# Chunked attention and a snake MLP in one kernel: the first batch's loads move to GpSimd, its units become even and odd blocks, its constants move to VectorE and ScalarE

## The chip, the cores and the metric

The kernel runs on one core of one Trainium2 chip. Its time is device microseconds of one execution; runs are summed up by their median. A profile is taken of one further execution: it shows five engines (TensorE as PE with its weight loads as PEld, VectorE as DVE, ScalarE as ACT, GpSimd as POOL, and SyncE as SP, which here only starts DMAs), 16 DMA engines that all queues share, and the clock that TensorE was granted. A "span" is the time from the first to the last instruction in the profile; the execution's own time is a little longer.

## The reference

Two parts, the second on the output of the first. Attention has batch 4, 8 heads, 768 rows and 64 columns a head; each chunk of 32 queries sees 16 rows to the left of its chunk, its own 32 and 8 to the right, and 8 memory rows of its batch:

```python
k_full = concatenate([mem_k, k[l_start:r_end]]); v_full = concatenate([mem_v, v[l_start:r_end]])
a = softmax(q_c @ k_full.T / sqrt(64))
out[c_start:c_end] = a @ v_full
```

The heads are laid side by side, which gives x of 3072 x 512. The MLP is

```python
h = x @ w_in                     # 512 -> 2048
s = sin(alpha * h)
g = h + s * s / (alpha + 1e-9)
y = g @ w_out                    # 2048 -> 512, float32, 3072 x 512
```

All inputs and the output are float32; the kernel computes the matmuls in bfloat16.

## The kernel before, in words

Everything is staged by batch. While the MLP of batch i runs on TensorE, the attention of batch i + 1 is worked in between. A first stage, number -1, has only the attention of batch 0 and the constants. What every engine does, and in which order, is written out by hand: `WORDS` holds one string for each stage, and each word calls one method of `Stage` (`do_` and the word's first letter). Every engine works through its own instructions in that order, so a wait of one instruction holds all behind it on its engine. There is no planner.

Words of the first stage that matter here, with what they issue:

- `k0` to `k3`, `l0` to `l3`: TensorE transposes a pair of heads of K or Q (`turn`, 12 matmuls each). `K1V`, `L0A`: the pair is copied from PSUM to its place by VectorE (V) or ScalarE (A).
- `s10`: scores of one unit (`u_scores`): head pair 1, half 0. A unit is two heads by four blocks of 96 queries. Two matmuls write the mask as a product of `mrow` and `mind`, eight add the scores, and ScalarE takes the exponential into a `pt` tile.
- `v10`: values of that unit (`u_values`, 8 matmuls), then `normed` on VectorE: a reciprocal of the sums and a product.
- `t10`, `T10`: four transposes and one copy of the result into xT, by VectorE or ScalarE.
- `V024`: V rows of heads 2 and 3 of batch 0 (`load_v`), two GpSimd DMAs that cast to bfloat16. V is kept in windows of 128 rows for each of 8 blocks: 64 rows, 8 memory rows, 56 rows.
- `dq068`: a pair of Q by GpSimd with a cast (`load_one`). `I02`, `I27`, `U69`: pieces of w_in and w_out, also by GpSimd.
- `a4A`: a cast of a float32 pair (`kq_f`) to bfloat16, by ScalarE.
- `C` and a letter: a group of constants (`const_b` and so on).
- `y1`, `z1`: fillers, TensorE matmuls on zeros (four of 128 columns, one of 512).

In the MLP's stages `b3` and `h3` are the two halves of the first layer's tile 3 (4 matmuls of 384 columns each, L457) with the sine on ScalarE after the second, `q3A` is the square, `g3` joins them on VectorE (L484), and `f6` takes six matmuls of the second layer (L495) from a queue.

The loads of batch 0 go two ways. Three of four pairs of K and of Q come as float32 on the queues of SP (K) and ScalarE (Q) into `kq_f`, and are cast by ScalarE or VectorE (`do_a`, L686). The fourth pairs and all of V come through GpSimd, which casts on the way. GpSimd, before its first load, writes the identity, zero rows of V's windows and `mind`. The first unit of a head pair takes blocks 0 to 3 and the second blocks 4 to 7, so V is needed whole by pairs. The program lets eight DMAs of GpSimd be in flight: each issue waits for the one eight before it.

The output of a batch is written by `close` in `second`: one DMA on SP for every 128 rows (L505).

Of the kernel before, what the change touches and what calls it, by code (L numbers as in the profile page):

```python
# [9 lines left out]
P = 128  # L10
QW = 96
# [15 lines left out]
    ),  # L27
    (
# [93 lines left out]
def kernel(  # L122
# [49 lines left out]
    pts = [consts.tile([P, H * QW + 32], BF, name=f"pt{i}") for i in range(NPT)]  # L172
# [6 lines left out]
    memk_bf = memv_st[0:NK, 0]  # L179
    memk_st = memv_st[96:104].rearrange("n b h d -> n b (h d)")  # L180
    memkT = consts.tile([P, HP, NK], BF, name="memkT")
# [36 lines left out]

    def win(vflat, row, n, height):
        a = vflat[row:row + 1, :]  # L220
        return bass.AP(tensor=a.tensor, offset=a.offset, ap=[[D, height], [QW * D, n], [1, D]])
# [20 lines left out]
    def put_memk(b):  # L242
        nc.vector.tensor_copy(
            kTs[b % 2][:, :, 24:856].rearrange("p g (j c) -> p g j c", c=104)[:, :, :, 40:40 + NM],
            memkT[:, :, NM * b:NM * b + NM].unsqueeze(2).to_broadcast([P, HP, NJ, NM]),
        )
# [100 lines left out]
    def u_scores(b, hp, half):  # L347
        t, bs = banks.pair()
        for e in range(2):
            nc.tensor.matmul(  # L350
                t[:, e, 0:HALF], mrow[64 * e:64 * e + 64, :],
                mind[64 * e:64 * e + 64, 4 * half:4 * half + 4].rearrange("p j m c -> p (j m c)"),
                start=True, stop=False,
            )
        for i in range(4):
            j = 4 * half + i
            for e in range(2):
                nc.tensor.matmul(
                    t[:, e, QW * i:QW * i + QW],
                    kTs[b % 2][64 * e:64 * e + 64, hp, 104 * j:104 * j + P],  # L360
                    qTs[b % 2][64 * e:64 * e + 64, hp, QW * j:QW * j + QW],
                    start=False, stop=(i == 3),
                )
        pt = next_pt()
        nc.scalar.activation(  # L365
            pt[:, 0:H * QW].rearrange("p (e c) -> p e c", e=2), t[:, :, 0:HALF],
            ACTF.Exp, scale=0.125,
        )
        banks.give(bs)
        return pt  # L370

    def u_values(b, hp, half, pt):
        ot, bs = banks.pair()
        otv = ot[:, :, 0:4 * (D + 1)].rearrange("p e (g c) -> p e g c", c=D + 1)
        for e in range(2):
            for i in range(4):
                nc.tensor.matmul(
                    otv[:, e, i, :], pt[:, HALF * e + QW * i:HALF * e + QW * i + P],
                    vws[b % 2][:, 2 * hp + e, 4 * half + i, 0:D + 1],
                )  # L380
        return normed(otv, bs)
# [109 lines left out]
    def second(i, gT, group=0):  # L491
# [8 lines left out]
        def close(o, bs, s, c0=0, c1=d_model):  # L500
# [4 lines left out]
            nc.sync.dma_start(out[S * i + P * s:S * i + P * s + P, c0:c1], o_sb[:, c0:c1])  # L505
# [30 lines left out]
    class Stage:  # L536
# [139 lines left out]

        def do_H(self, a):
            put_memv_heads(int(a))
# [3 lines left out]

        def do_a(self, a):
            hp = int(a[0]) % HP
            dst = kq[int(a[0]) // HP]
            copier(a[1])(  # L686
                dst[:, 2 * hp:2 * hp + 2].rearrange("p h r d -> p h (r d)"), kq_f[int(a[0])][:]
            )
# [53 lines left out]
    kq_f = [mlp.tile([P, 2, 6 * D], F32, name="kq_f", tag=t) for t in ("u", "s2") * 4]  # L742
# [3 lines left out]

    def load_f(ring, src, hp, t):
        ring.dma_start(
            t[:], src[0, 2 * hp:2 * hp + 2].rearrange("h (p r) d -> p h (r d)", p=P)
        )  # L750
# [5 lines left out]
    for hp in range(HP - 1):  # L756
        load_f(nc.sync, k, hp, kq_f[hp])
        load_f(nc.scalar, q, hp, kq_f[4 + hp])
        if hp == 0:
            nc.sync.dma_start(memv_f[64:72], mem_v[0].rearrange("h n d -> n h d"))  # L760
    nc.vector.memset(zeros[:], 0.0)
    nc.vector.memset(tiny[:], 0.0)
    nc.vector.memset(mcol[:], 0.0)
    masks.make_identity(nc, ident[:])
    for vw in vws:
        nc.gpsimd.memset(vw[0:32, 0, 0, 0:D], 0.0)
        nc.gpsimd.memset(vw[96:128, H - 1, NJ - 1, 0:D], 0.0)
# [29 lines left out]
    def const_i():  # L797
        nc.gpsimd.tensor_tensor(out=asum[:, 0:5], in0=ident[:, 0:5], in1=ident[:, 64:69], op=ALU.add)
        nc.gpsimd.tensor_tensor(out=asum[:, 5:7], in0=asum[:, 0:3:2], in1=asum[:, 3:5], op=ALU.add)
        nc.gpsimd.tensor_copy(  # L800
            mind[:], asum[:, 0:3].unsqueeze(1).unsqueeze(3).to_broadcast([P, NJ, 3, 32])
        )
        nc.gpsimd.tensor_copy(mind[:, 0, 0, :], asum[:, 5:6].to_broadcast([P, 32]))
        nc.gpsimd.tensor_copy(mind[:, NJ - 1, 2, :], asum[:, 6:7].to_broadcast([P, 32]))

    def const_k():
        nc.vector.tensor_copy(memk_bf, memk_f[0:NK])
        bank, bs = banks.single()
        mt = bank[:, 0:2 * NK].bitcast(BF).rearrange("p (g c) -> p g c", g=HP)
        for g in range(HP):  # L810
            nc.tensor.transpose(
                mt[:, g, :], memk_bf[:, 2 * g:2 * g + 2, :].rearrange("p e d -> p (e d)"),
                ident[0:NK, 0:NK]
            )
        nc.vector.tensor_copy(memkT[:], mt)
        put_memk(0)
        if not CROSSED[1][0]:
            put_memk(1)
        banks.give(bs)

    def const_f():
        nc.vector.tensor_copy(memv_st[64:72, 0], memv_f[64:72])

    def const_l():
        nc.vector.tensor_copy(ident_f[:], ident[0:FT, 0:FT])
# [7 lines left out]
    def const_z():  # L833
        for kT in kTs:
            nc.gpsimd.memset(kT[:, :, 0:16], 0.0)
            nc.gpsimd.memset(kT[:, :, 848:856], 0.0)

    def const_p():
        for pt in pts:
            nc.gpsimd.memset(pt[:, H * QW:H * QW + 32], 0.0)  # L840

    def const_v():
        for vw in vws:
            nc.gpsimd.memset(vw[:, :, :, D:D + 1], 1.0)

    def const_s():
# [3 lines left out]
    consts_of = dict(b=const_b, f=const_f, m=const_m, i=const_i, k=const_k, l=const_l, p=const_p, v=const_v,  # L850
                     s=const_s, z=const_z)
# [37 lines left out]
```

## Time and profile before

| | us |
|---|---|
| median of 3 runs | 214.56 |
| lowest and highest | 214.24, 215.09 |
| the profiled execution's own time | 214.68 |
| its span | 212.8 |

| engine | busy us | share of the span |
|---|---|---|
| PE | 204.9 | 96% |
| ACT | 143.7 | 68% |
| DVE | 139.9 | 66% |
| POOL | 100.9 | 47% |

In a row of a timeline come the start in us from the span's start, the length in us, the engine (a small q behind it is its sequencer, which starts DMAs), the line of the code, the operation with out<-in, shape and count, and in brackets how long the engine stood idle before and what ended that. In a row of the waits come who waited, for whom, and the total in us, the times and the longest. In a group's row come busy time in us and the mean of one in ns, and after the second bar idle time before them. In a row of DMA issues come the queue, the count, the size of each at its destination, and the us from issue to landing. In a row of a DMA queue come packets, MB written, and the time of its packets as a share of 16 engines.

### The profile page before, as it was taken

The page shows a single profiled execution, that of the slowest core. Times are in us where ns is not written, and L with a number is a line of the kernel's source. Part 1 is how long each engine was busy: PE and PEld are TensorE (multiplying, and loading weights), DVE is VectorE, ACT ScalarE, POOL GpSimd, SP SyncE. Part 2 cuts the span into 40 slices and gives each one's busy share as a digit, 9 for nine tenths or more (in the row PEclk, how much of TensorE's full clock was granted, in tenths as well). Part 3 has the DMA queues.
Part 4 walks back from the last instruction along what each step waited for, and adds up shares of the span by engine and source line. Part 5 has one row for each costly group of instructions (what it writes and reads, how often), then busy time and mean ns, then how long its engine had stood idle before and what let it go on. Part 6 is the DMA issues. An engine that isn't in the chain of part 4 may idle for free.

```text
span 212.8 us, 4568 instructions
## 1 busy us (share of the span) xinstructions
PE 204.9 (96%) x1772; PEld 118.1 (55%) x1772; DVE 139.9 (66%) x210; ACT 143.7 (68%) x229; POOL 100.9 (47%) x142
## 2 busy tenths in 40 slices
PE   7879999999999999999999999999999999999994
PEld 7456665565455556555455555554555555554453
DVE  4788788999452749976766649897247187865010
ACT  2579898978848469968837199887856189891110
POOL 8998605589697297109795048664000022200000
PEclk9999999999999999999999999999999999999999
DMA  5999999999999999999999259999944400000312
GB/s 156 332 158 139 212 207 204 205 139 183 131 160 155 176 114 129 121 144 146 146 152 183 74 125 125 137 157 133 134 104 107 137 0 0 3 2 0 148 52 99
DMA packets 95853, 27.82 MB, mean 131 GB/s; under 512 B 84808, under 2 KB 92376, under 8 KB 95832
## 3 DMA queue, kind: packets, MB, share of 16 engines
q0 software_dynamic: 69152, 13.64, 89.3%
q1 hardware_dynamic: 25720, 12.68, 29.6%
q10 hardware_dynamic: 960, 1.21, 1.7%
q8 instruction: 14, 0.23, 0.6%
q14 instruction: 7, 0.06, 0.1%
HBM read 29.66 MB, written 6.29 MB: 169 GB/s over the span
## 4 chain that ended last, share of the span: by engine, by line
PE 78%; DVE 8%; ACT 5%; DMA 4%; issue 3%; SPq 1%; DVEq 0%; ACTq 0%
PE ps L495 39%; PE ps L457 30%; DMA kq_f<-in_k_dram 4%; PE ps L447 3%; DVE gT L484 2%; PE ps L418 2%; DVE x_blk L387 2%; DVE s L480 2%; ACT s L477 2%; PE ps L399 1%; ACT pt L365 1%; PE ps L312 1%; ACT u L472 1%; DVE q_bf L686 1%; DVE rinv L386 0%
## 5 line engine op out<-in xcount | busy, mean ns | idle before, releaser
L495 PE MATMUL ps<-w_out_sb,gT 128*128 128x512 bf16 (+1 forms) x400 | 89.1, 371 | 0.0
L457 PE MATMUL ps<-xT,w_in_sb 128*128 128x384 bf16 x512 | 85.9, 326 | 0.6 <-DVE gT L484 0.4
L484 DVE SCALAR_TENSOR_TENSOR gT<-s,inv_alpha,ps 128x768 bf16<-128x768 f32 x64 | 63.1, 1012 | 12.3 <-ACT s L477 5.2
L457 PEld LDWEIGHTS <-w_in_sb 128*128 128x128 bf16 x512 | 49.7, 98 | 35.2 <-issue 2.0
L472 ACT ACTIVATE u<-ps,alpha_sb 128x768 f32<-128x768 f32 x64 | 56.6, 894 | 16.9 <-PE ps L457 14.4
L495 PEld LDWEIGHTS <-gT 128*128 128x128 bf16 x400 | 37.1, 98 | 37.1 <-DVE gT L484 0.2
L480 POOL TENSOR_TENSOR s<-u 128x768 f32<-128x768 f32 x11 | 17.2, 1568 | 67.2 <-ACT u L472 56.4
L432 ACT ACTIVATE pt<-ps,biasm 128x256 bf16<-128x256 f32 x72 | 27.1, 488 | 10.5 <-PE ps L418 10.5
L502 DVE COPY o_sb<-ps 128x512 f32<-128x512 f32 (+1 forms) x15 | 10.0, 669 | 27.6 <-PE ps L495 25.7
L480 DVE TENSOR_TENSOR s<-u 128x768 f32<-128x768 f32 x23 | 21.9, 953 | 7.6 <-ACT u L472 7.5
L477 ACT ACTIVATE s<-u 128x768 f32<-128x768 f32 x30 | 25.0, 841 | 0.5
L387 DVE TENSOR_TENSOR x_blk<-ps,rinv 96x512 bf16<-96x512 f32 x32 | 22.0, 687 | 1.1
L502 ACT COPY o_sb<-ps 128x512 f32<-128x512 f32 (+1 forms) x10 | 5.7, 572 | 22.0 <-PE ps L495 22.0
L208 POOL DMA_DIRECT2D vw<-in_v_dram x13 | 12.0, 926 | 6.3 <-PE ps L399 5.4
L386 DVE RECIPROCAL rinv<-ps 96x8 f32<-96x8 f32 x32 | 6.4, 199 | 13.1 <-PE ps L447 12.7
L215 POOL DMA_DIRECT2D vw<-in_v_dram x13 | 13.3, 1024 | 1.6 <-DMA vw<-in_v_dram 1.6
L274 POOL DMA_DIRECT2D kst<-in_k_dram x16 | 13.0, 815 | 1.8 <-DMA vw<-in_v_dram 1.2
L268 POOL DMA_DIRECT2D kst<-in_k_dram x16 | 11.1, 691 | 2.1 <-DMA kst<-in_k_dram 1.0
L281 POOL DMA_DIRECT2D q_bf<-in_q_dram x12 | 10.7, 911 | 0.0
L402 ACT COPY xT<-ps 128x384 bf16<-128x384 bf16 x10 | 5.0, 496 | 8.2 <-PE ps L399 8.2
L447 PEld LDWEIGHTS <-pt 128*128 128x128 bf16 x192 | 8.2, 97 | 4.2 <-ACT pt L432 0.3
L447 PE MATMUL ps<-vw,pt 128*128 128x65 bf16 x192 | 8.9, 193 | 0.0
(83 smaller groups left out, 140.7 us busy)
## 6 DMA issues: line engine op xcount, KB each, us to landing
out_dram<-o_sb SPq DMA_DIRECT2D x23, 256.0 KB, 2.2
q_bf<-in_q_dram POOLq DMA_DIRECT2D x12, 128.0 KB, 7.7
kq_f<-in_k_dram SPq DMA_DIRECT2D x3, 384.0 KB, 6.2
kq_f<-in_q_dram ACTq DMA_DIRECT2D x3, 384.0 KB, 7.9
w_in_sb<-in_moe_w_in_dram POOLq DMA_DIRECT2D x1, 1152.0 KB, 12.9
vw<-in_v_dram POOLq DMA_DIRECT2D x7, 128.0 KB, 7.7
vw<-in_v_dram POOLq DMA_DIRECT2D x8, 112.0 KB, 8.1
kst<-in_k_dram POOLq DMA_DIRECT2D x14, 64.0 KB, 5.5
```

What stands on the lines that cost most here:

```text
L215: nc.gpsimd.dma_start(vw[72:128, c0:hi, 0:D], win(vflat, base + QW * c0 + 48, hi - c0, 56))
L274: nc.gpsimd.dma_start(kst[72:72 + n, j, :].rearrange("p (h d) -> p h d", d=D), k[b, :, QW * j + 48:QW * j + 48 + n, :].rearrange("h p d -> ...
L387: nc.vector.tensor_tensor(out=x_blk[:].rearrange("p g e d -> p e g d"), in0=otv[0:QW, :, :, 0:D], in1=rinv[:].unsqueeze(3).to_broadcast([Q ...
L432: nc.scalar.activation(pt[:, 0:H * QW].rearrange("p (g e c) -> p g e c", g=2, e=4)[:, :, :, 32 * m:32 * m + 32], sc[:, :, 0:4 * QW].rearra ...
L447: nc.tensor.matmul(otv[:, e, hp, :], pt[:, QW * i:QW * i + P], vws[b % 2][:, 2 * hp + e, j, 0:D + 1],)
L457: nc.tensor.matmul(t["hT"][:, hf, 0:HALF], w_in_sb[:, kt, P * t["ft"]:P * t["ft"] + P], t["xT"][:, kt, HALF * hf:HALF * hf + HALF], start= ...
L472: nc.scalar.activation(t["u"][:], t["hT"][:, :, 0:HALF], ACTF.Sin, scale=alpha_sb[:, ft:ft + 1])
L477: nc.scalar.activation(s2[:], u[:], ACTF.Square)
L480: e.tensor_tensor(out=s2[:], in0=u[:], in1=u[:], op=ALU.mult)
L484: nc.vector.scalar_tensor_tensor(out=gT[:, ft, :].rearrange("p (e c) -> p e c", e=2), in0=t["s2"][:], scalar=inv_alpha[:, ft:ft + 1], in1= ...
L495: nc.tensor.matmul(o[:, c0:c1], gT[:, ft, P * s:P * s + P], w_out_sb[:, ft, c0:c1], start=(ft == 0), stop=(ft == FT - 1),)
L502: copier(state["engines"][state["o"] % len(state["engines"])])(o_sb[:, c0:c1], o[:, c0:c1])
```

## The change

It touches stage -1, the words of stage 0, and the output's row order of batch 0.

- All pairs of K and Q of batch 0 are loaded by GpSimd with the cast, in the order pair by pair with V; the first load is POOL's first instruction. The float32 tiles, the loads on SP and ScalarE, and the casts go.
- The two units of a head pair are the even and the odd blocks. The last pair's V is loaded in such halves (`load_v_half`, words `G030` and `G031`). xT of batch 0 holds the even blocks first, and `close` puts the rows back in order with two DMAs for each 128 rows.
- `asum`, the identity's memset, and the zeros and ones that batch 0 needs are made by VectorE, `mind` by ScalarE; those of batch 1 stay on GpSimd and come later (`Cw`, `Cy`). The eight `pt` tiles become one, so that one memset serves them.
- Memory keys are transposed as float32 and go from PSUM straight to kT; memory values go from float32 to V's windows by pairs (`put_memv_first`, words `n0A` and so on) instead of a cast and one broadcast copy.
- The words of stages -1 and 0 are ordered anew, with fewer fillers: 44 of 128 columns and one of 512 in place of 48 and 14.

```diff
-        'y1 y1 y1 Ci y1 a4A We y1 Cb a1A y1 y2 y1 y1 dq068 Cl y1 Cm y1 Cf z1 z1 eVA z1 eVA a0A Ck m0 Cz z1 '
-        'dk068 Cp V024 z1 z1 V002 z1 a2V V068 z1 z1 Cv l0 z1 a5V z1 L0A k1 k0 z1 k2 l1 K1A V046 K0A a6V L1A '
-        's00 s10 s11 K2V l2 k3 L2V K3A s01 v11 dm l3 L3A v10 s20 v01 s30 v00 s31 v30 s21 v31 z1 T01 v20 T30 '
-        'I02 Cs T00 v21 t10 T20 t31 z1 t11 I27 t21 Ws '
+        'Cv Cp Cb dk002 dq024 y1 y1 Ci We y1 dk024 y1 y1 y1 n0A y1 k0 K0A V002 Cz y1 Cd y1 n1V dq046 dk046 Ck '
+        'Cm l0 L0A k1 s00 l1 V024 s01 K1V L1V v00 y1 n3A s10 v01 l2 k2 n2A T01 s11 K2V dq068 dk068 z1 V046 '
+        'L2V G030 T00 v10 y1 v11 s20 l3 s21 k3 L3V K3V Cw T10 v20 s30 G031 v21 Cy I02 s31 v30 T11 v31 t20 T21 '
+        'I27 Cs Ws t30 Cl dm t31 '
...
-        'o8 b0 h0 I7g q0V U69 U12 b1 h1 dq108 q1A b4 h4 b3 g0 h3 b6 g1 dk108 q4V g4 q3A b2 h2 h6 b5 h5 Ufg g3 '
-        'b7 q2V U01 U56 q6P h7 g2 q5A b10 U24 q7P g6 h10 b9 q10A g5 h9 U45 b8 h8 g7 g10 q8A q9V V158 b11 h11 '
+        'o8 b0 h0 I7g q0V U69 U12 Ws b1 h1 dq108 q1A b3 b4 g0 h4 h3 b6 g1 q4V g4 q3A dk108 b2 h2 h6 b5 h5 Ufg '
+        'g3 b7 q2V U56 q6P h7 g2 q5A b10 U24 q7P g6 U01 h10 b9 q10A g5 h9 U45 b8 h8 g7 g10 q8A q9V V158 b11 '
...
+    def load_v_half(b, hp, half):
...
+        c0 = 2 * hp * NJ + half
...
+        c1 = (2 * hp + 2) * NJ
+        for c, r0, r1 in ((lo, 0, 64), (c0, 72, 128)):
+            row = b * H * S + QW * c - 16 + (r0 if r0 == 0 else 64)
+            a = vflat[row:row + 1, :]
+            nc.gpsimd.dma_start(
+                vw[r0:r1, c:c1:2, 0:D],
+                bass.AP(tensor=a.tensor, offset=a.offset,
+                        ap=[[D, r1 - r0], [2 * QW * D, (c1 - c + 1) // 2], [1, D]]))
...
-                mind[64 * e:64 * e + 64, 4 * half:4 * half + 4].rearrange("p j m c -> p (j m c)"),
+                mind[64 * e:64 * e + 64, half:NJ:2].rearrange("p j m c -> p j (m c)"),
...
-            j = 4 * half + i
+            j = 2 * i + half
...
+            if i:
+                nc.sync.dma_start(out[S * i + P * s:S * i + P * s + P, c0:c1], o_sb[:, c0:c1])
+                return
+            r = 0
+            while r < P:
+                at = P * s + r
+                n = min(P - r, QW - at % QW)
+                g = at // QW
+                row = QW * (2 * (g % 4) + g // 4) + at % QW
+                nc.sync.dma_start(out[row:row + n, c0:c1], o_sb[r:r + n, c0:c1])
+                r += n
...
-    for hp in range(HP - 1):
-        load_f(nc.sync, k, hp, kq_f[hp])
-        load_f(nc.scalar, q, hp, kq_f[4 + hp])
...
+    nc.vector.memset(ident[:], 0.0)
+    load_one(q, q_bf, 0, 0, 2)
+    masks.make_identity(nc, ident[:], nomemset=True)
...
+        nc.scalar.copy(mind[:], asum[:, 0:3].unsqueeze(1).unsqueeze(3).to_broadcast([P, NJ, 3, 32]))
...
-        nc.vector.tensor_copy(memkT[:], mt)
-        put_memk(0)
...
+        for b in range(B):
+            if not CROSSED[b][0]:
+                put_memk(b, mt, "V")
```

More of the change, by code (lines that the diff above doesn't have):

```diff
@@ L171 @@
     NPT = 8
-    pts = [consts.tile([P, H * QW + 32], BF, name=f"pt{i}") for i in range(NPT)]
+    pt_all = consts.tile([P, NPT, H * QW + 32], BF, name="pt")
+    pts = [pt_all[:, i] for i in range(NPT)]
     memv_st = consts.tile([P, B, H, D], BF, name="memv_st")
@@ L675, in do_m, with do_n, do_G @@
             put_memv(int(a))
+        def do_n(self, a):
+            put_memv_first(int(a[0]), a[1])
+        def do_G(self, a):
+            load_v_half(*(int(c) for c in a))
         def do_H(self, a):
@@ L797, in const_i, with const_d @@
     def const_i():
[L798 to L804, printed above, removed]
+        nc.vector.tensor_tensor(out=asum[:, 0:5], in0=ident[:, 0:5], in1=ident[:, 64:69], op=ALU.add)
+        nc.vector.tensor_tensor(out=asum[:, 5:7], in0=asum[:, 0:3:2], in1=asum[:, 3:5], op=ALU.add)
+        nc.scalar.copy(mind[:], asum[:, 0:3].unsqueeze(1).unsqueeze(3).to_broadcast([P, NJ, 3, 32]))
+        nc.scalar.copy(mind[:, 0, 0, :], asum[:, 5:6].to_broadcast([P, 32]))
+        nc.scalar.copy(mind[:, NJ - 1, 2, :], asum[:, 6:7].to_broadcast([P, 32]))
+    def const_d():
+        nc.vector.tensor_copy(ident_f[:], ident[0:FT, 0:FT])
     def const_k():
[L807 removed]
         bank, bs = banks.single()
[L809 removed]
+        mt = bank[:, 0:HP * NK].rearrange("p (g c) -> p g c", g=HP)
         for g in range(HP):
             nc.tensor.transpose(
[L812 to L818 removed]
+                mt[:, g, :], memk_f[0:NK, 2 * g:2 * g + 2, :].rearrange("p e d -> p (e d)"),
+                ident_f[0:NK, 0:NK]
+            )
+        for b in range(B):
+            if not CROSSED[b][0]:
+                put_memk(b, mt, "V")
         banks.give(bs)
[L821 to L822 removed]
     def const_l():
[L825 removed]
         bank, bs = banks.single()
```

65 lines of the change are left out of this document (31 added, 34 removed), and 6 rows, old and new, of the table WORDS.

## The prediction

> **What bounds the kernel now.** I read the page first, then the waits of TensorE over the whole run, the chain in order of time, and the timelines of the first 45 us.
>
> ```profile
> span 212.8 us, 4568 instructions
> ...
> PE   7879999999999999999999999999999999999994
> ```
> ```profile
> PE ps L725 <- DVE tiny L762: 1.2, 1, 1.2
> PE ps L312 <- DVE q_bf L686: 1.0, 1, 1.0
> PE ps L811 <- DVE memv_st L807: 0.9, 1, 0.9
> ```
> ```profile
> 2.57 8.45 DMA kq_f<-in_k_dram
> ...
> 14.60 2.22 ACT pt L365 x3
> ...
> 24.95 2.62 PE ps L457 x16
> ```
> ```profile
> 1.20 4.45 PE L725 MATMUL ps<-zeros 128*128 128x128 bf16 x40 [1.20 <-DVE tiny L762]
> ...
> 8.29 1.47 PE L719 MATMUL ps<-zeros 128*128 128x512 bf16 x6
> ...
> 10.69 0.86 PE L312 MATMUL ps<-ident,k_bf 128*64 128x128 bf16 x24
> ...
> 19.08 0.34 PE L350 MATMUL ps<-mind,mrow 64*128 64x384 bf16 x2
> 19.25 0.33 PE L358 MATMUL ps<-qT,kT 64*128 64x96 bf16 x8
> 19.52 0.43 PE L377 MATMUL ps<-vw,pt 128*128 128x65 bf16 x8
> ...
> 24.78 17.40 PE L457 MATMUL ps<-xT,w_in_sb 128*128 128x384 bf16 x104
> ```
> ```profile
> 26.28 0.90 ACT L472 ACTIVATE u<-ps,alpha_sb 128x768 f32<-128x768 f32 x1
> ```
>
> The three largest waits of TensorE come to 3.1 us of a 212.8 us span, and all three lie in the first batch's preparation. The chain starts with 8.45 us of waiting for K's float32 loads, passes to the exponentials at 14.60, and reaches the first layer (L457) at 24.95; the timeline has that layer from 24.78 with 104 matmuls in 17.40, 167 ns each, without a gap. Behind it the slices stand at 9 to the end. So some 188 us are a queue of matmuls that no other engine holds up, and the time is the moment at which the first layer starts plus those 188. The change keeps the matmuls of the three later batches and all MLP matmuls. What it is worth is how far the first layer moves. Its first tile has 8 matmuls (24.78 + 8 x 0.167 = 26.1), and the first sine follows at 26.28; that is the mark I work out.
>
> **The loads.** Four groups of rows, POOL's timeline and the DMA view of single issues:
>
> ```profile
> 1.03 0.29 POOL masks.py:199 TENSOR_SCALAR_AFFINE_SELECT ident<-ident 128x128 bf16<-128x128 bf16 x1
> ...
> 3.66 0.94 POOL L191 DMA_DIRECT2D q_bf<-in_q_dram  x1
> ...
> 6.91 0.89 POOL L215 DMA_DIRECT2D vw<-in_v_dram  x1
> 7.78 0.56 POOL L204 DMA_DIRECT2D vw<-in_v_dram  x1
> ...
> 15.78 0.81 POOL L249 DMA_DIRECT2D w_in_sb<-in_moe_w_in_dram  x1
> ```
> ```profile
> q_bf<-in_q_dram POOLq DMA_DIRECT2D x1, 192.0 KB, 7.8
> ```
> ```profile
> w_in_sb<-in_moe_w_in_dram POOLq DMA_DIRECT2D x1, 256.0 KB, 6.9
> ```
> ```profile
> w_in_sb<-in_moe_w_in_dram POOLq DMA_DIRECT2D x1, 640.0 KB, 8.1
> ```
> ```profile
> vw<-in_v_dram POOLq DMA_DIRECT2D x1, 64.0 KB, 2.6
> ```
> ```profile
> q0 software_dynamic: 543, 0.41, 131.5%
> ```
> ```profile
> q0 software_dynamic: 2514, 0.30, 241.6%
> ```
>
> The last two are GpSimd's queue in two stretches of 2 us: rows of Q at 35 to 37 (0.41 MB, 205 KB a us) and rows of V at 12 to 14 (0.30 MB, 150 KB a us). A pair of heads of K or Q (192 KB) thus takes 0.95 us of DMA, all eight 7.6. V (64 blocks of 120 rows of 128 B, 0.98 MB) takes 6.6; I take 7.9, since it slowed in the stretch after. Together 15.5 us.
>
> POOL's program now opens with the first load of Q at 0.75, where it had its identity. Issues cost 0.94 at most, 0.85 on average; the identity slips in between (0.29). Ahead of the last V half stand 4 x 0.85 + 0.29, the 48-row V load 0.56, then two K/Q pairs of 1.7, six V issues of 0.88, four half-block issues that have no row and lie between 0.56 and 0.89 (I take 0.7), and two memsets (0.65): it is issued by 17. DMA work starts about 2.0 (below) and needs 15.5, so POOL and the DMA engines end together: last K/Q pair landed by 14, the last V by 18.6, w_in's first part (issued about 17.3) by 20.1, against 15.78 + 6.9 = 22.7 before. The in-flight limit on this queue (each issue waits for the one eight earlier) finds landings one to five us old.
>
> How long the first issue waits for its first packet has no clean row. The 64 KB V load at 73.3, into a quiet queue, landed after 2.6; the first Q load of before, behind six float32 loads on the other queues, after 7.8. I take the near end, since those six are gone: Q's first pair lands at 3.4, K's at 4.5. The far end is a rival.
>
> **The compute of the first batch.** Durations by form, 0 to 26 us:
>
> ```profile
> L365 ACT ACTIVATE pt<-ps 128x768 bf16<-128x768 f32 x8 | 6.3, 822 | 0.2 <-PE ps L358 0.2
> L387 DVE TENSOR_TENSOR x_blk<-ps,rinv 96x512 bf16<-96x512 f32 x8 | 5.5, 687 | 0.3
> ...
> L332 ACT COPY qT<-ps 128x768 bf16<-128x768 bf16 x3 | 2.5, 819 | 1.4 <-PE ps L312 1.4
> ...
> L386 DVE RECIPROCAL rinv<-ps 96x8 f32<-96x8 f32 x8 | 1.6, 198 | 0.4 <-PE ps L377 0.4
> ...
> L402 DVE COPY xT<-ps 128x384 bf16<-128x384 bf16 x4 | 1.1, 344 | 0.0
> ...
> L332 DVE COPY qT<-ps 128x768 bf16<-128x768 bf16 x1 | 1.0, 958 | 0.6 <-PE ps L312 0.6
> L323 DVE COPY kT<-ps 128x768 bf16<-128x768 bf16 x1 | 0.9, 939 | 0.0
> ...
> L800 POOL COPY mind<-asum 128x768 bf16<-128x768 bf16 x1 | 0.8, 818 | 0.0
> ...
> L822 DVE CAST memv_st<-memv_f 8x512 bf16<-8x512 f32 x1 | 0.6, 584 | 0.0
> ```
> ```profile
> 3.33 0.24 POOL L803 COPY mind<-asum 128x32 bf16<-128x32 bf16 x1
> ```
> ```profile
> 7.14 0.20 ACT L738 ACTIVATE tiny<-zeros 1x1 f32<-1x1 bf16 x1
> ```
> ```profile
> 1.35 0.75 DVE L773 TENSOR_REDUCE biasm<-ident 128x1 f32<-128x56 bf16 x6
> ...
> 3.35 0.15 DVE L786 TENSOR_TENSOR mcol<-biasm 128x2 bf16<-128x2 f32 x1
> ```
>
> *Constants.* The identity is ready at 0.75 + 0.94 + 0.29, about 2.05, where it was 1.35. VectorE's mask constants (1.35 to 3.5, 2.15 us) end at 4.2, two additions for asum (as L786, 0.15 each) at 4.5. Then ScalarE writes mind: 0.82 on POOL, taken the same, plus two small copies of 0.24 and the exponential's warm-up of 0.2: 6.05. Its first memory-value copy (8 partitions x 1024, float32) has no row; twice L822 gives 1.17, a 128x768 ScalarE copy scaled by size 1.1; below it cannot be free, so 0.5 to 1.2, and I take 1.1: 7.15. K's first pair goes out at 7.15 to 7.9, Q's to 8.7. The data has been there since 4.5 and the transposes (24 in 0.86) since 7, so late loads have 1.2 us of slack. The GpSimd constants taken away (mind, 8 pt memsets, vw, kT) cost POOL nothing now; their replacements on VectorE before 2.05 hide behind the wait for the identity. The casts (L686) go; nothing takes their place but these two copies.
>
> *First unit.* Its scores take 0.34 (L350 and L358, each 0.17 from start to start) and end at 9.1, its exponential 0.8 (9.9). The transposes of Q's second pair stand behind these scores in TensorE's order, so VectorE copies it from 9.55 to 10.5.
>
> *VectorE from 10.5 on* has its work queued without a gap that I can find: eight units of 0.69 + 0.20 + 0.03 (0.92, 7.4 us) and four copies of K and Q pairs (0.95, 3.8 us): 21.7. Then three copies to xT (0.36 with issue) and alpha's copy and reciprocal (0.42): 23.2. ScalarE beside it has from 9.1 eight exponentials (6.4), two memory copies (2.2) and three xT copies (1.5) ahead of the last unit's values: 20.0 with its waits, 0.4 ahead of VectorE's need. The last V half (18.6) is 1.5 ahead of its use, w_in's first part (20.1) 2 ahead. So VectorE, not the loads, ends the stage. TensorE's first tile ends at 23.4 against 26.1: **2.7 us earlier.**
>
> *Later.* w_in's next part, issued behind it, lands about 23.3 (before 17.64 + 8.1 = 25.7); it is wanted at 22.1 + 16 x 0.167 = 24.8. The loads behind it move with it by some 2.5. Batch 0's output takes twelve issues on SP instead of six; they stand ahead of the DMA transposes of batch 1 in SP's order, but each waits for a copy that TensorE's 16 matmuls release, so SP has time between them: nothing. If that cover is gone, the transposes of c6, c4 and c2 are what comes late. The even/odd order in matmul operands is a stride on 96-column runs: nothing.
>
> Sum: the profiled execution took 214.68, 1.9 over its span and 0.12 over the median of the runs shown (214.56); 214.68 - 2.7 = 212.0, which I give also against the median.
>
> **The rivals.**
>
> *Late first packet.* If GpSimd's first load needs the far end's wait, everything that arrives moves by 3.2; 1.2 is slack, 2.0 is paid: gain 0.7, 214.0. For it: the 7.8. Against it: six loads on other queues stood before that one.
>
> *The weights do not move.* If w_in's second part still lands at 25.7, TensorE waits 0.9 to 1.1 at its third tile: gain 1.6, 213.1. Against it: the same bytes, begun earlier.
>
> *TensorE stays slow: slower than before.* The first 40 fillers took 111 ns per 128 columns, the later ones 245 per 512, 61 per 128: at the start TensorE runs at about half pace. After the change 28 fillers end at about 4.3, and then TensorE waits for K's first pair; if it stays at half pace until 12, the eight blocks of work there on which VectorE waits (five transposes of 0.45, three scores of 0.34, two values of 0.4 (L377), 4.1 us) double: about +4.0, less the 2.7 gained: 216.0. It decides from 2.7 us of such loss on. For it: twelve 512-column fillers are gone. Against it: K lands at 4.5, and from there to 7 TensorE has work.
> The Trainium skill, "TensorE: Matmul & The Clock Gate", Part 1, says that the clock is halved by default, comes up after a busy window of about 3.4 us and falls back after an idle one. The 111 and 61 ns agree with its two states; by that rule a gap shorter than the window would cost nothing, and with late loads the gap would be as long as the window.
>
> *It does nothing.* If VectorE's work runs a quarter longer, because in the new order it reads PSUM beside ScalarE and TensorE all the time, its 11.2 us become 14.0 and the gain is gone: 214.8. In the rows above its eight units ran beside ScalarE's exponentials already, at 0.69.
>
> **How the numbers follow.** 0.5% is 1.07 us, about what a measurement of this kernel tells from no change. My forecast (gain 1.8 to 3.8, 210.9 to 212.8) has 0.52; weights not moving 0.12; late packet or nothing gained 0.19; slow TensorE 0.17. So faster 0.64, same 0.19, slower 0.17. The unknown copies (0.5 to 1.2, three of them, two off the path) and half-block issues set the low end: 210.8. The high end, 215.8, reaches into the slow case.
>
> **What would show it.** Right: first K transposes by 5.5, first exponential about 9, VectorE without gaps from 10.5 to 23, first-layer matmuls from about 22 without a gap, a load of w_in landed by 20.5, granted clock 1.0 throughout. Wrong: Q's first packet after 5 us; granted clock 0.5 after 6 us; TensorE waiting for DMA in the first layer; GpSimd issues above 1 us.

## The result and the profile after

| | before | after |
|---|---|---|
| median, us (same chip) | 214.82 | 217.12 |
| lowest and highest | 214.24, 215.33 | 216.69, 217.39 |
| ratio to before, with its 95% interval | | 1.0106 [1.0071, 1.0140] |
| the profiled execution, and its span | 214.68, 212.8 | 216.69, 214.9 |

The change makes the kernel about 1% slower, where 2.7 us less was forecast. Measured again beside other kernels it took 216.24, ratio 1.0075 [1.0042, 1.0109]. A ratio is to the kernel before on the same chip, with its 95% interval, and leaves out executions more than 1.5% above their kernel's fastest, so it can differ a little from that of two medians.

The line of the clock from the profile's page, and the first 16 us of TensorE's timeline:

```profile
PEclk9669999999999999999999999999999999999999
```
```profile
1.21 2.99 PE L758 MATMUL ps<-zeros 128*128 128x128 bf16 x28 [1.21 <-DVE zeros L784]
6.79 0.53 PE L336 MATMUL ps<-ident,k_bf 128*64 128x128 bf16 x12 [2.60 <-DMA k_bf<-in_k_dram]
7.25 1.03 PE L758 MATMUL ps<-zeros 128*128 128x128 bf16 x8
8.22 0.60 PE L834 MATMUL ps<-ident_f,memk_f 16*128 16x16 f32 x4
8.75 0.29 PE L816 MATMUL ps<-ident,mcol 128*128 128x128 bf16 x1
8.97 0.85 PE L336 MATMUL ps<-ident,q_bf 128*64 128x128 bf16 x12
...
15.01 0.50 PE L336 MATMUL ps<-ident,k_bf 128*64 128x128 bf16 x12
```

TensorE stands idle for 2.60 us until K's first pair lands. Twelve transposes take 0.53 us at 6.79, 0.85 at 8.97 and 0.50 again at 15: between 7.3 and 14.1 it runs at half pace, the two sixes in the clock's line. Q's first transposes come 2.2 us behind K's, since eight fillers, the memory keys and a constant stand between them in TensorE's order.

GpSimd's timeline and the DMA view of its first two loads and of w_in's first part:

```profile
1.27 0.93 POOL L190 DMA_DIRECT2D q_bf<-in_q_dram  x1 [0.82 <-POOLq L896]
2.29 0.31 POOL masks.py:199 TENSOR_SCALAR_AFFINE_SELECT ident<-ident 128x128 bf16<-128x128 bf16 x1
2.54 0.73 POOL L190 DMA_DIRECT2D k_bf<-in_k_dram  x1
...
17.36 1.52 POOL L273 DMA_DIRECT2D w_in_sb<-in_moe_w_in_dram  x2
```
```profile
q_bf<-in_q_dram POOLq DMA_DIRECT2D x1, 192.0 KB, 3.5
k_bf<-in_k_dram POOLq DMA_DIRECT2D x1, 192.0 KB, 4.2
```
```profile
w_in_sb<-in_moe_w_in_dram POOLq DMA_DIRECT2D x1, 256.0 KB, 5.6
```

Q's pair lands at 1.27 + 3.5 = 4.8, K's at 2.54 + 4.2 = 6.75, w_in's first part at 17.36 + 5.6 = 22.95. ScalarE, VectorE and TensorE up to the first layer:

```profile
5.83 1.04 ACT L267 CAST vw<-memv_f 8x1024 bf16<-8x1024 f32 x1
7.36 0.80 ACT L347 COPY kT<-ps 128x768 bf16<-128x768 bf16 x1 [0.50 <-PE ps L336]
9.86 0.80 ACT L356 COPY qT<-ps 128x768 bf16<-128x768 bf16 x1 [1.70 <-PE ps L336]
11.26 0.81 ACT L389 ACTIVATE pt<-ps 128x768 bf16<-128x768 f32 x1 [0.59 <-PE ps L382]
```
```profile
13.41 0.20 DVE L410 RECIPROCAL rinv<-ps 96x8 f32<-96x8 f32 x1 [0.34 <-PE ps L401]
...
25.46 0.29 DVE L426 COPY xT<-ps 128x384 bf16<-128x384 bf16 x1
```
```profile
25.05 5.20 PE L481 MATMUL ps<-xT,w_in_sb 128*128 128x384 bf16 x31
```

The first exponential stands at 11.26, 3.3 ahead of the 14.60 of before, and the first layer at 25.05, 0.27 behind the 24.78 of before. In this execution the other 1.8 us go later. TensorE's waits over the run, two pieces of the chain in order of time (start, length), and the queue of SP before and after:

```profile
PE ps L442 <- DMA qT<-q_bf: 1.0, 1, 1.0
PE ps L442 <- DVE o_sb L526: 0.5, 1, 0.5
```
```profile
2.54 4.22 DMA k_bf<-in_k_dram
...
94.12 8.59 DMA qT<-q_bf
```
```profile
76.09 9.87 SPq L296 DMA_TRANSPOSE kT<-kst  x6
86.06 10.73 SPq L299 DMA_TRANSPOSE qT<-q_bf  x6
```
```profile
76.77 10.83 SPq L320 DMA_TRANSPOSE kT<-kst  x6
87.69 11.57 SPq L323 DMA_TRANSPOSE qT<-q_bf  x6
```

The transposes of batch 2's K and Q begin 0.7 later and take 22.4 us in place of 20.6, so the scores at 102 us find Q's last part missing. Where the chain of before had one stretch of DMA, K's loads, this one has two.

### The profile page after: what moved, and what is told of

Read it like the earlier page. It is cut to its first block, busy times and chain, and to the rows that moved or that the text cites. A ratio compares the mean times of both kernels' runs of the same rounds, so it can differ in the third digit from the quotient of the medians.

```text
span 214.9 us, 4532 instructions
## 1 busy us (share of the span) xinstructions
PE 204.4 (95%) x1755; PEld 118.1 (55%) x1755; DVE 137.7 (64%) x215; ACT 144.0 (67%) x231; POOL 102.5 (48%) x130
## 4 chain that ended last, share of the span: by engine, by line
PE 66%; SPq 8%; DMA 8%; DVE 7%; ACT 5%; issue 4%; POOL 1%; DVEq 0%; POOLq 0%; ACTq 0%
PE ps L519 34%; PE ps L481 21%; SPq L320 5%; DMA qT<-q_bf 4%; SPq L323 3%; DVE gT L508 2%; PE ps L336 2%; PE ps L471 2%; DMA out_dram<-o_sb 2%; PE ps L442 2%; DMA k_bf<-in_k_dram 2%; DVE s L504 2%; DVE x_blk L411 1%; ACT u L496 1%; ACT s L501 1%
## 5 line engine op out<-in xcount | busy, mean ns | idle before, releaser
L410 DVE RECIPROCAL rinv<-ps 96x8 f32<-96x8 f32 x32 | 6.4, 199 | 14.1 <-PE ps L471 13.1
L207 POOL DMA_DIRECT2D vw<-in_v_dram x12 | 11.0, 919 | 8.2 <-PE ps L423 5.5
L298 POOL DMA_DIRECT2D kst<-in_k_dram x16 | 11.8, 737 | 3.6 <-DMA vw<-in_v_dram 3.3
L292 POOL DMA_DIRECT2D kst<-in_k_dram x16 | 11.8, 737 | 2.9 <-DMA vw<-in_v_dram 1.6
L214 POOL DMA_DIRECT2D vw<-in_v_dram x12 | 11.6, 964 | 1.1 <-DMA vw<-in_v_dram 1.1
L426 ACT COPY xT<-ps 128x384 bf16<-128x384 bf16 x11 | 5.5, 498 | 8.6 <-PE ps L423 8.5
```

The source lines that it names most:

```text
L292: nc.gpsimd.dma_start(kst[r0:64, j, :].rearrange("p (h d) -> p h d", d=D), k[b, :, lo + r0:lo + 64, :].rearrange("h p d -> p h d"),)
L298: nc.gpsimd.dma_start(kst[72:72 + n, j, :].rearrange("p (h d) -> p h d", d=D), k[b, :, QW * j + 48:QW * j + 48 + n, :].rearrange("h p d -> ...
```

## The experiments

"First layer" is the start of its first matmul, "first exponential" that of ScalarE's first one; both are of one profiled execution, while median and ratio are of 4 to 12; e16 to e18 are one execution each.

**Fillers, and the words of stage 0.** The changed kernel with more fillers ahead of K's transposes, with before's words in stage 0, and with both:

```diff
 e1   -y1 y1 y1 n0A y1 k0 K0A      +y1 y1 y1 n0A y12 k0 K0A
 e15  -y1 y1 y1 n0A y1 k0 K0A      +y1 y1 y1 n0A y6 k0 K0A
 e2   WORDS[1] as in the kernel before
 e9   e1 and e2 together
```

> The changed kernel with eleven more groups of four 128-column fillers between the first 28 fillers and the first transposes of K, so that TensorE has no gap before K's first pair lands at 6.8. Nothing else moves. If the halved clock (granted 0.5 from 7.3 to 14.1) made the first unit late: granted clock 1.0 from about 4 on, first exponential at about 10 instead of 11.3, first layer from 23.5 to 24.3 instead of 25.05, time 215.6 to 216.4 against 217.1 of the changed kernel. If K's landing and VectorE's queue rule and the clock does not matter: first layer at 25.0 and 217.1.

> The changed kernel with five more filler groups ahead of K's first transposes in place of eleven, so that they end before K lands in most executions. Theory: the fillers help because TensorE does not idle long enough to lose its clock; then five groups give as much as eleven, 214.7 to 215.3, and the granted clock is 1.0 from 8 us on. Rival: what helped was something else that the eleven groups delay; then it lies between the changed kernel and that with eleven, 215.5 to 216.5.

> The changed kernel with the words of stage 0 as they were before the change; stage -1 and all else as changed. In the changed kernel the last values of batch 1 stand two second-layer matmuls later, and GpSimd's V loads and SP's transposes behind them began 0.4 to 0.6 later; TensorE then waited 1.0 for Q's transposes at 102 and 0.5 for a copy at 115, and lost 1.8 between 101 and 116. If the new order of words is the cause: these waits go and the time is 215.3 to 215.7. If the twelve output DMAs on SP are the cause: still 216.8 to 217.3.

> The changed kernel with two edits at once: eleven more groups of four 128-column fillers ahead of K's first transposes, and stage 0's words as in the kernel before. Theory: the changed kernel loses at two separate places, the first batch at half clock and the wait on Q's transposes at 102 us; then the two edits add up, about 214.3 (ratio 1.000 to 1.001), with no wait on a DMA or on o_sb between 100 and 117. Rival: the fillers help only because they take away the same wait (the first layer's start and the SP queue move together); then nothing is added to what the fillers alone gave, about 215.0 (ratio 1.002 to 1.004).

| | median | ratio | first exponential | first layer |
|---|---|---|---|---|
| e1, eleven groups more | 214.97 | 1.0024 [0.9995, 1.0052] | 11.16 | 24.73 |
| e15, five groups more | 214.76 | 1.0023 [0.9995, 1.0051] | 10.24 | 23.81 |
| e2, old words | 216.20 | 1.0083 [1.0050, 1.0115] | 10.99 | 24.78 |
| e9, eleven groups and old words | 214.82 | 1.0025 [1.0000, 1.0050] | 10.87 | 24.26 |

e15, TensorE's timeline:

```profile
6.92 0.53 PE L336 MATMUL ps<-ident,k_bf 128*64 128x128 bf16 x12 [1.37 <-DMA k_bf<-in_k_dram]
7.38 0.62 PE L758 MATMUL ps<-zeros 128*128 128x128 bf16 x8
7.93 0.42 PE L834 MATMUL ps<-ident_f,memk_f 16*128 16x16 f32 x4
...
8.44 0.53 PE L336 MATMUL ps<-ident,q_bf 128*64 128x128 bf16 x12
```

The wait for K is still there (1.37), but the eight fillers take 0.62 in place of 1.03 and nothing behind runs at half pace. Five groups give as much as eleven: between 1.0023 and the changed kernel's 1.0075 and 1.0106 lie 0.5 to 0.8%, 1.1 to 1.8 us. So about 70 to 80% of the measured loss goes with the pace of TensorE in the first 14 us; what is left, 0.2%, cannot be told from none in e1 and e15. The old words give nothing that can be told from the changed kernel, although in e2's profiled execution the waits at 102 and 115 us are gone; nor do they give anything on top of the fillers. The theory of two losses that add up fell.

In e1's profiled execution, its slowest (216.42), K's pair lands only at 7.8, so its late first exponential is no measure of full pace; e15's is, with K at 6.88. From one execution to another this landing differs by more than a microsecond: 6.6 in e7, 8.2 in e11. In e15 the next bound shows: the chain back from the first layer leads to V rows of the second pair of heads (start, length).

```profile
9.64 6.11 DMA vw<-in_v_dram
```

They land at 15.76, and 8.05 us later the first layer starts. Of the 0.97 by which it is ahead of before, 0.62 is left at the last first-layer matmul.

**Six outputs; twelve outputs alone.** e3 puts batch 0's xT in natural order in the changed kernel, so six output DMAs serve; e4 gives the kernel before twelve.

```diff
 e3  -xT[:, hp, HALF * half:HALF * half + HALF].rearrange("p (g c) -> p g c", g=4)
     +xT[:, hp, :].rearrange("p (g e c) -> p g e c", g=4, e=2)[:, :, half, :]
     and close's single dma_start as before
 e4  +            while r < P:
     +                n = min(P - r, QW - (P * s + r) % QW)
     +                nc.sync.dma_start(out[P * s + r:P * s + r + n, c0:c1], o_sb[r:r + n, c0:c1])
     +                r += n
```

> The changed kernel with xT of batch 0 in natural order (each unit's four blocks are written 192 columns apart), so that the output goes out in six DMAs of 128 rows again. If the twelve output DMAs on SP are the cause of the loss between 101 and 116: the waits there go and the time is 215.3 to 215.8 (the first layer's first half needs both units of the last pair, up to 0.4 later). If the order of the words is the cause: 216.8 to 217.5.

> The kernel before with each of batch 0's six output DMAs split in two, at the same rows as in the changed kernel; nothing else. If twelve outputs delay SP's transposes: 216.0 to 216.6 against 214.8, with TensorE waiting for Q's transposes near 102. If they are hidden: 214.5 to 215.1 and no such wait.

e3: 216.50, ratio 1.0109 [1.0048, 1.0170], of four executions. e4: 214.86, 1.0019 [0.9993, 1.0045]. Twelve outputs cost nothing that can be told from none, and taking them back mends nothing.

**The changed kernel again, Q ahead of K, and a mixture.** e6 puts `l0 L0A` ahead of `k0 K0A`; e7 adds five filler groups and the old words of stage 0.

```diff
 e6  -n0A y1 k0 K0A ... Ck Cm l0 L0A k1     +n0A y1 l0 L0A k0 K0A ... Ck Cm k1
 e7  as e6, with -L0A k0 +L0A y5 k0, and WORDS[1] as before
```

> The changed kernel once more, beside the three that follow on one chip. Both theories: 2.0 to 2.7 us above the kernel before (ratio 1.009 to 1.012).

> The changed kernel with Q's first pair transposed and copied ahead of K's first pair (word order l0 L0A k0 K0A; the fillers stay where they are), since Q lands at 4.8 and K at 6.7. In the changed kernel Q's transposes stood behind K's, eight fillers and two constants, and its copy by ScalarE began at 9.9. If the place of Q's transposes in TensorE's order is what made the first unit late: first scores at about 8.7 instead of 10.4, first exponential at 9.5, first layer 1.3 to 1.8 earlier, time 215.3 to 216. If the halved clock alone is: first exponential at 10.3 to 11, time 216.3 to 217.

> The changed kernel with Q's first pair ahead of K's, five groups of four fillers in the gap between them, and the words of stage 0 as before the change. If clock, order of Q and the words of stage 0 each cost their own part: granted clock 1.0 from 7 on, first exponential at 9 to 9.5, first layer at 23 to 23.5, time 0.5 to 1.5 below the kernel before. If the loads' pace sets the stage: first layer at 24.5 to 25 and a time 0 to 0.6 above the kernel before.

e5: 216.24. e6: 216.20, 1.0092 [1.0064, 1.0120]; Q is copied at 6.88 in place of 9.86, yet the first exponential comes at 10.69 and the first layer at 24.88, with TensorE at half pace from 8.5 to 15.4. e7: 215.14, 1.0040 [1.0011, 1.0069]; first exponential 11.82, first layer 24.96. The first layer is where the rival had it, but not by the loads' pace: in its profiled execution the added fillers run at half pace themselves (20 in 2.31 us), and K's transposes stand behind them until 7.96. Q's place alone is not what holds the stage.

**Before without its early fillers; before with the new words.** e8 leaves out the nine `z1` ahead of `l0` in stage -1 of the kernel before; e10 and e16 (the same kernel) give it the new words of stage 0.

```diff
 e8   -Cf z1 z1 eVA z1 eVA a0A Ck m0 Cz z1 dk068 Cp V024 z1 z1 V002 z1 a2V V068 z1 z1 Cv l0
      +Cf eVA eVA a0A Ck m0 Cz dk068 Cp V024 V002 a2V V068 Cv l0
 e10  WORDS[1] of the changed kernel in the kernel before
```

> The kernel before without the nine 512-column fillers ahead of the first transposes of Q, so that TensorE has little to do from 6.6 to 9.7. If a gap of that length halves the clock and the halved clock is what such a gap costs: granted clock 0.5 in some stretch after 6, first layer 0.5 to 2 later, time up to 2 above the kernel before. If the clock does not matter at this place: time as the kernel before, within 0.4.

> The kernel before with nothing but the new order of stage 0's words. Theory: that order alone brings Q's transposes (L299) too late, since c2 and c4 stand earlier against the values' loads or later against TensorE; then a wait on qT of 0.5 to 1.0 appears near 102 us and the time is 215.3 to 216.0 (ratio 1.004 to 1.008). Rival: the order costs nothing by itself and needs the later start of GpSimd's loads, or the twelve outputs on SP; then 214.2 to 214.8 (ratio 1.000 to 1.002) and no such wait.

> The kernel before with nothing but the new order of stage 0's words, one more profiled execution. Theory: with the first layer at its old place (24.0 to 24.9) the new words bring no wait on Q's transposes near 102 us, so the first and last first-layer matmul stand as far apart as in the kernel before, within 0.4 us. Rival: the wait comes with the words alone in some executions, 0.5 us or more.

e8: 214.71, 1.0018 [0.9989, 1.0047], first layer 24.04, though the granted clock was 0.5 from 8.2 to 11.6. In the kernel before, what TensorE does there is not waited for (its first exponential comes at 13.4 to 14.7); half pace cost only where the next step stood behind it. e10: 214.89, 1.0028 [1.0011, 1.0045]; e16, one execution: 214.13. In neither profile does TensorE wait on qT between 98 and 118 us. The new words alone thus cost 0.1 to 0.45%, between the theory and its rival, and no run shows where.

**Two copies off VectorE; first pairs as float32.** e11 is e9 with two of Q's copies on ScalarE; e12 is e11 with K's and Q's first pairs on SP's and ScalarE's queues as float32, cast by VectorE and ScalarE.

```diff
 e11  -l1 V024 s01 K1V L1V v00      +l1 V024 L1A s01 K1V v00
      -s21 k3 L3V K3V               +s21 k3 L3A K3V
 e12  +    for ring, src, t in ((nc.sync, k, kq_f[0]), (nc.scalar, q, kq_f[1])):
      +        ring.dma_start(t[:], src[0, 0:2].rearrange("h (p r) d -> p h (r d)", p=P))
      -n0A y12 k0 K0A               +n0A y12 a0V a1A k0 K0A
```

> As the one with fillers and old words, and the copies of Q's second and last pairs to qT (L1V, L3V) go to ScalarE, which takes 1.9 us off VectorE. Theory: VectorE's queue, 12.3 us without a gap in the changed kernel, ends the first stage; then the first layer starts at 23.5 to 24.2 instead of 24.7 to 25.1, and the time falls by 0.7 to 1.3 against the kernel without this edit. Rival: the landing of the last loads (V's last half at 20.9, the first part of w_in at 22.95) or TensorE ends it; then it falls by 0.3 at most and VectorE has idle gaps of 1 us or more in sum behind its first norm.

> As the one with the two copies on ScalarE, and the first pairs of K and Q come as float32 on SP's and ScalarE's queues as they did before, cast by VectorE and ScalarE; GpSimd starts with the second pairs. Theory: the late landing of GpSimd's first two loads (4.8 and 6.8 us) holds the first exponential at 11; then it falls to 9.0 to 10.0, and the time by another 0.5 to 1.2. Rival: the first exponential is not what VectorE's queue waits on, or float32 pairs and casts come no earlier; then the first exponential stays above 10.4 and the time within 0.4 of the kernel without this edit.

e11: 215.03, 1.0037 [1.0021, 1.0053]. e12: 214.78, 1.0039 [1.0019, 1.0060]. Rows of e11 on ScalarE, VectorE and TensorE:

```profile
11.61 0.81 ACT L389 ACTIVATE pt<-ps 128x768 bf16<-128x768 f32 x1 [0.43 <-PE ps L382]
```
```profile
17.85 0.20 DVE L410 RECIPROCAL rinv<-ps 96x8 f32<-96x8 f32 x1 [0.80 <-PE ps L401]
...
20.38 0.96 DVE L347 COPY kT<-ps 128x768 bf16<-128x768 bf16 x1 [0.78 <-PE ps L336]
```
```profile
25.27 1.79 PE L481 MATMUL ps<-xT,w_in_sb 128*128 128x384 bf16 x10
```

VectorE now stands idle, and still 13.66 us pass from the first exponential to the first layer (e12: 10.34 to 23.99, 13.65). In e9, without the edit, it is 13.39, in the changed kernel 13.79. So VectorE's queue, though full, is not alone the bound, even if the last 4.5 us of e11's chain are VectorE's (20.38 to 24.88): scores, exponentials, values, norms and transposes hand over to each other in the written order, and taking 1.9 us from one engine shows as waits on the others. e12's exponential came at 10.34, above the 10.0 expected: eleven filler groups ended at 7.0 and K's transposes stood behind them. Its first layer is 1.28 ahead of e11's, its median only 0.25 below.

**Early data, with and without fillers.** e13 is e12 with five filler groups more in place of eleven, Q's first pair right behind K's, the first memory values on VectorE, and e11's copies back on VectorE; e14 is e13 with no more fillers than the changed kernel.

```diff
 e13  -n0A y12 a0V a1A k0 K0A V002 ... n1V     +a0V a1A y6 k0 K0A l0 L0A V002 ... n0V n1V
 e14  -a1A y6 k0                               +a1A y1 k0
```

> The changed kernel with the first pairs of K and Q as float32 on SP's and ScalarE's queues, cast by VectorE and ScalarE; five more filler groups ahead of K's transposes, so that they end near 6 us, when the cast is done; Q's first pair right behind K's; memory values of the first pairs by VectorE; stage 0's words as before; Q's copies on VectorE as in the changed kernel. Theory: in the changed order the first layer starts 13.1 to 13.8 us after the first exponential, whatever delayed that one (10.3 to 12.0 in the runs so far), and everything behind follows; then the first exponential comes at 8.8 to 9.6, the first layer at 22.2 to 23.3, and the time is 212.6 to 213.8, below before. Rival: the loads, V's last half or w_in, end the first stage once the exponential is earlier; then TensorE waits on a DMA between 18 and 27 us, the first layer starts no earlier than 23.6, and the time is 214.2 to 215.0.

> As the one before it, with one filler group ahead of K's transposes instead of six, so that TensorE stands idle from about 4.3 until the cast is done near 6. Theory: it is the idle gap in front of K's first pair that brings the half clock; with a gap of 1.5 to 2 us at full or half clock, up to 1.2 us later first layer and 0.5 to 1.5 us more time than with the fillers. Rival: fillers and clock cost nothing when the data is early; then both are within 0.4 us of each other.

e13: 213.98, 0.9979 [0.9953, 1.0006], the lowest median here, not told apart from before. e14: 215.73, 1.0037 [1.0005, 1.0068]. Rows of e13 on ScalarE and TensorE, and its issue of w_in's second part (at 16.87):

```profile
9.47 1.70 ACT L389 ACTIVATE pt<-ps 128x768 bf16<-128x768 f32 x2 [1.27 <-PE ps L382]
```
```profile
22.61 2.77 PE L481 MATMUL ps<-xT,w_in_sb 128*128 128x384 bf16 x16
25.96 3.26 PE L481 MATMUL ps<-xT,w_in_sb 128*128 128x384 bf16 x19 [0.59 <-DMA w_in_sb<-in_moe_w_in_dram]
...
46.80 1.34 PE L519 MATMUL ps<-w_out_sb,gT 128*128 128x512 bf16 x5 [0.31 <-DMA w_out_sb<-in_moe_w_out_dram]
...
53.35 1.89 PE L519 MATMUL ps<-w_out_sb,gT 128*128 128x512 bf16 x8 [0.24 <-DMA w_out_sb<-in_moe_w_out_dram]
```
```profile
w_in_sb<-in_moe_w_in_dram POOLq DMA_DIRECT2D x1, 640.0 KB, 9.0
```

The first exponential and the first layer come where the theory put them; the first layer is 2.17 us ahead of before. Then TensorE waits for w_in's second part, landed at 16.87 + 9.0 = 25.9 (before 17.64 + 8.1 = 25.7), and twice for w_out. Against before, the lead of a first-layer matmul falls from 2.17 to 1.42 at the third tile and to 0.30 at 75 us. Both sides of the expectation held in part: the chain moved, and the loads took the gain. e14's first exponential is at 10.94, its first layer at 24.85, so without the fillers its early first pairs brought nothing. One row of e14 shows that this is not the pace alone:

```profile
9.29 0.85 PE L336 MATMUL ps<-ident,k_bf 128*64 128x128 bf16 x12 [1.16 <-DMA k_bf<-in_k_dram]
```

The twelve transposes are at half pace (its clock fell at 7.84), and before them TensorE waits 1.16 us for K's second pair, which landed at 9.25 where e13 has 7.88.

**The changed kernel once more, and with old words.**

> The changed kernel with the old words of stage 0, one more profiled execution, since its median (216.2) lies 0.8 above its profiled one. Theory: executions in which TensorE stays at half clock longer, or K lands later, start the first layer later, 25.2 to 26.5, and the rest follows; no wait on qT near 102 us. Rival: the first layer stands at 24.7 to 25.1 again and the time goes at waits further on, 1 us or more in sum.

> The changed kernel, one more profiled execution, for the split of its loss. Theory: first layer at 24.9 to 26 and a wait of 0.5 to 1.5 us on qT near 102 us, together 1 to 3 us over the kernel before. Rival: no such wait, and the whole loss ahead of the first layer.

e18 is the changed kernel, one execution of 215.52; TensorE's timeline, and one stretch of 2 us with the clock:

```profile
1.20 3.17 PE L758 MATMUL ps<-zeros 128*128 128x128 bf16 x28 [1.20 <-DVE zeros L784]
6.95 0.85 PE L336 MATMUL ps<-ident,k_bf 128*64 128x128 bf16 x12 [2.58 <-DMA k_bf<-in_k_dram]
7.73 1.03 PE L758 MATMUL ps<-zeros 128*128 128x128 bf16 x8
...
12.41 0.50 PE L374 MATMUL ps<-mind,mrow 64*128 64x384 bf16 x2
...
13.72 0.34 PE L374 MATMUL ps<-mind,mrow 64*128 64x384 bf16 x2
```
```profile
8.00:10.00 2.00, 2.00 (x25) 1.65 (x24) 0.66 (x2) 0.64 (x1) 2.00 (x4) 1.00 2.08 148
```

The 28 fillers take 113 ns each, the pace of the first fillers of every run, and half pace lasts until about 13. The granted clock of the stretch (third number from the end) reads 1.00, but this trace has no record of the clock before 13.07, where it becomes 1.0, and a stretch without a record reads as 1.00. So here TensorE did not fall back in the gap; it had not come up before it. The first layer starts at 25.51, and there is no wait on qT at 102 us. e17 (old words, 215.72) shows the same: first record at 12.31, half pace until 12.4, first layer 25.22. Of the three profiled executions of the changed kernel two have the wait on qT (1.0 and 0.7 us). e1 has 0.3 of it; the kernels with old words, and before with the new ones, none. It was seen only with the new words and where SP's transposes began at 76.8 or later, and not always there (e18: 77.2; e3: 78.2); together those twelve took 19 to 22 us from one execution to another. How often it comes was not settled.

**All runs side by side.** Without added fillers the changed kernel and its variants stand at 1.0075 to 1.0109 (the change, e2, e3, e5, e6); with fillers that kept full pace at 1.0023 to 1.0025 (e1, e9, e15). The first stage as it was before started the first layer at 24.02 to 24.88 in four profiled executions (before, e4, e10, e16), as changed at 24.78 to 25.51 in five (the change, e2, e5, e17, e18): on average 0.7 later, so the single pair with 0.27 shows less than the usual delay. The rest of the loss lies further on and differs from one execution to another; how much of that follows from the late start was not settled.

## Why the prediction was wrong, point by point

- **The likeliest sum failed at its first steps.** GpSimd's first issue was put at 0.75 and came at 1.27; I took the near end of the landing, 2.6 us, where the rows show 3.5 and 4.2. In the profile after K's first pair landed 2.25 us after the forecast 4.5, nearly twice the slack of 1.2. The last V half landed at 16.44 + 4.5 = 20.9 (forecast 18.6), w_in's first part at 22.95 (20.1; before 22.7). Only the first pairs came earlier than before; the last V had landed at 14.28 + 7.1 = 21.4 there, so the last loads gained 0.5 or nothing. The rival *Late first packet* thus came true in part: Q's pair was 1.4 late and K's 2.25, where it had 3.2, a figure that the prediction does not work out (its two landings, 7.8 and 2.6, differ by 5.2). By itself this delay cost little: K's copy began at 7.36 for 7.15.
- **A term was missing.** Between K's and Q's first transposes TensorE has fillers, memory keys and a constant: from K's start to Q's 1.5 us at full pace (e15, 6.92 to 8.44), 0.46 of them K's own. I had Q's copy right behind K's, at 7.9; it came at 9.86. With K there at 4.5 this work would have been over by 4.5 + 1.5 = 6.0, ahead of both copies; with K at 6.75 it stands between them. So the late landing and the missing term cost together what neither costs alone. The memory copy was right (1.04 for 1.1, at 5.83; the terms given for 6.05 add up to 6.00). At full pace the first exponential is at 10.24 (e15), 1.1 behind the forecast 9.1; in the profiled executions at half pace (the change, e2, e5, e17, e18) at 11.0 to 12.0.
- **Where the miss of 4.7 us lies** (216.69 against 212.0): the first layer came at 25.05 for 22.1, 2.95 late. Of this 2.2 stand ahead of the first exponential, 1.1 by the late landing and the missing term and 1.0 by half pace (11.26 against e15's 10.24), and 0.8 behind it, where 13.0 us were forecast and 13.79 measured. The last 1.8 are the waits further on. So two steps failed, the first exponential at 9.1 and the claim that everything behind the first layer moves with it; the stretch between them was nearly right.
- **"VectorE ends the stage"**: its 12.7 us from first norm to last copy were right in size (13.41 to 25.75, 12.3), but it was not the only bound (e11 against e9).
- **The rival that TensorE stays slow was the right one**, with 0.17. Its 216.0 was 1.1 below the 217.12, and near the 216.24 measured again, by luck, since its parts were wrong: I priced half pace at +4.0 against a gain of 2.7; the runs show 1.1 to 1.8 for the pace (e1, e9 and e15 against the change and e5) and next to nothing gained. My argument against it, that K lands at 4.5, fell with the loads. By the Trainium skill, "TensorE: Matmul & The Clock Gate", Part 1, the clock falls back after an idle window of about 3.4 us, from which I took it that a shorter gap costs nothing. The gap here was 2.6 us and the pace fell, at 7.29; it also fell in e14 with a gap of 1.62 and in e8 with none above 1.21 between the clock's rise at 4.75 and its fall at 8.16, while e15's 1.37 did no harm. So a gap shorter than 3.4 us can cost the pace, and its length alone does not decide it; what does is open. The measurement decides.
- **"The weights move with it" failed** where it mattered: w_in's second part lands at 26.05 after and 25.9 in e13, against 25.7 before. That rival's mechanism (0.12) is what e13 meets once the stage is early. Its price of 0.9 to 1.1 was for w_in alone, and e13 waits 0.59 there; the waits on w_out, 0.31 and 0.24, it did not have, and by 75 us 1.87 of the lead are gone.
- **"The time is the first layer's start plus 188"** holds for small moves only. With 2.17 us of lead e13 keeps 0.3; with 0.27 of delay the profiled changed kernel ends 2.1 later, mostly by the waits at 102 and 115 us.
- **Twelve outputs, "nothing"**, held for the time within 0.45% (e4). What came late in the profile after was not c6, c4 and c2 but batch 2's K and Q transposes.
- **The stride of even and odd blocks** cost nothing: at full pace the scores' matmuls take 203 ns each in both orders (L358 before, L382 in e1).

## What to carry to other kernels

When loads move to another queue, carry the landing of the first ones through the sum as a range between the near and the far row (here 2.6 and 7.8; it was 3.5 and 4.2), and list every instruction that stands between them and the first step that waits. Ask what TensorE does until the data lands: a few filler matmuls that bridge the gap were worth 1.1 to 1.8 us here. Before saying that everything behind an earlier start moves with it, compare the landing of each later load with its new due time. Where several engines hand a unit back and forth in a fixed order, less work on the fullest one need not shorten the chain.

## What the runs showed of the hardware

- A granted clock of 1.00 in a view is no proof of full pace: in e18 twelve transposes took 0.85 us at 6.95 and eight fillers 1.03, as in the stretch of the profile after that shows 0.50, while the view shows 1.00, because the trace's first record of the clock stands at 13.07. The pace is read from the durations.
- TensorE was at half pace in the first 14 us in two ways. In the profile after and in e5 the clock came up at 3.87 and 4.20, before the gaps of 2.6 and 3.1 us, and fell at 7.29 and 7.62; it stayed down for 6.8 and 3.4 us, although TensorE was busy almost without a break behind the gap. In e18 and e17 it came up for the first time at 13.07 and 12.31.
- GpSimd's first load, its first instruction of the kernel's text, was issued at 1.27. The first two loads took 3.5 and 4.2 us to land, with two more issued behind them at 3.26 and 3.97, against 2.6 for a 64 KB load into the same queue at 73 us.
